# Causal convolution and spectral mix: x with two rows to a partition, and the convolution cut into quadrants of the array

## The chip, the cores and the metric

The kernel runs on one core of a Trainium2 chip. The metric is the device time of one execution in microseconds (us). Before the change the median of three runs is 177.64 us (177.45 to 178.16). A profiled execution gives the trace; its own time and span stand in the table below.

A core has five engines, each with its own queue: TensorE (PE in the profile; its weight loads are PEld), VectorE (DVE), ScalarE (ACT), GpSimd (POOL) and SyncE (SP). TensorE writes to eight banks of PSUM; VectorE and ScalarE move ("evict") results from PSUM to SBUF. Transfers run on 16 DMA engines; POOL issues the input transfers, which also turn float32 into bfloat16, and SP issues the output.

## The reference

```python
# x (8, 3264, 192); weight (8, 7); w_r, w_i (64, 192, 192); w_ch (192, 192)
w = softmax(weight, axis=-1)                          # 8 heads, 7 taps
x_pad = concat(zeros(B, 6, D), x)                     # causal
x = einsum('hk,bskhg->bshg', w, windows(x_pad))       # 24 columns per head
X = rfft(x, axis=1)[:, :64]                           # 64 modes
Yr = Xr @ w_r - Xi @ w_i                              # per mode
Yi = Xr @ w_i + Xi @ w_r
y = irfft(Y, n=S, axis=1)
u = x + y
out = u + maximum(u @ w_ch, 0)
```

## The kernel before

Batches go in four pairs `q`. A row block is 256 sequence rows; there are 13 to a batch (the last has 192), so 26 half blocks `t` of 128 rows or fewer. `xall` holds x in bfloat16 in slots of half blocks, both batches of a pair side by side, 192 columns each.

*Loading.* `load_unit` (L148) loads one unit of a pair in two transfers, one per batch. One x row goes to one partition: the packet is one row, 192 bfloat16, 384 bytes in SBUF. The short tails of all pairs come in two transfers (L236). The units are (first block, blocks): `UNITS0 = (0,2) (2,3) (5,4) (9,4)` for the first pair and `UNITS = (0,4) (4,4) (8,5)` for the others, 13 units in all. After x and `w_ch` POOL issues the mode weights (`load_w`, L264), two transfers of 288 KB for each of 16 groups of four modes. Eight groups have room from the start; each of the other eight is asked for once `mix(g)` of an earlier group has run.

*Front.* VectorE builds the banded tap matrix `band` (masks L178, softmax L180 to L190, seven predicated copies L193, copies to `band` L199 on ScalarE and L201 on VectorE). Meanwhile 30 filler products (`NIDLE`, L174) keep TensorE busy.

*Convolution.* `conv_pass` takes two heads of one unit: 16 products (L283) of a 128-row by 64-column tile of the array, two column halves side by side, into a PSUM tile of two banks. There are three such tiles in turn. The result goes back in place to `xall`, alternately through ScalarE (L290) and VectorE (L292); the rows come out so that even and odd rows lie in separate half blocks. Four passes make a unit.

*Fourier tables.* `table(step, t0, t1)` computes the cosines and sines in `ftab`: steps 0 to 2 on VectorE (L210, L213, L215), 3 to 5 on ScalarE (L217, L219, L221). The dictionary `extra` places these steps between the passes, in three parts of the table.

*Transform.* `dft` (L301) adds up the transform of a pair over its 26 half blocks, in two column halves of the array, in one of two banks kept for it. `dfts(n)` places five or six half blocks at a time between the passes. ScalarE copies the sum to `xs` (L305). `xtrans` (L316, L318) transposes it, and L325 and L327 copy it to `xt`.

*Mode products.* `mix(g)` (L426) multiplies four modes by their weights. Around it `some(n)` works off a list of transposes (L387, copied by L377 and L379) that the output stage needs. `mix(0)` needs the transform of all four pairs. Near the end `warm` (L580) puts filler products between the last mode products.

*Output stage.* From about 106 us products (L642), clamps (L558), additions (L545) and output transfers run interleaved over the 26 half blocks of each pair. The change doesn't edit it.

The order of instructions on each engine is the program's order (`manual_schedule`); only the waits are added by the framework.

Of the kernel before, what the change touches and what calls it, by code (L numbers as in the profile page):

```python
# [19 lines left out]
def kernel(  # L20
# [18 lines left out]
    NF = S // P  # L39
    HALF = S - NF * P  # L40
    NB = NF // 2 + 1
    NT = 2 * NB
    PL = (S - 2 * P * (NB - 1)) // 2
    NSLOT = NQ * NT + 1
    PW = 32 + KK - 1
    TWOPI = 6.283185
    MAGIC = 12582912.0
    NIDLE = 30
    UNITS0 = ((0, 2), (2, 3), (5, 4), (9, 4))
    UNITS = ((0, 4), (4, 4), (8, 5))  # L50
# [20 lines left out]
    band = shared[:, 0:H * 2 * P].rearrange("p (h c) -> p h c", h=H)  # L71
# [4 lines left out]
    ylate = sb("ylate", [2 * D], BF16)  # L76
# [5 lines left out]
    xs = [sb(f"xs{i}", [2, D], BF16) for i in range(2)]  # L82

# [21 lines left out]
    packed = temp(H * PW, BF16)  # L105
# [6 lines left out]
    wrec = temp(H, F32)  # L112
    cidx = temp(PW, F32)
    goff = temp(1, F32)
    masks = temp(KK * PW, U16)
# [20 lines left out]
    zl = open_psum("left", (2, 2))  # L136
    zr = open_psum("right", (1, 1, 2))
    ZC = [zl[0], zl[1], zr[2]]
    zf = zr[0:2]

    def load_unit(q, b0, n):
        t0 = 2 * b0
        nf = min(2 * n, NF - t0)
        s0 = NT * q + t0 + 1
        for i in range(2):
            off = ((2 * q + i) * S + P * t0) * D
            src = bass.AP(tensor=x.tensor, offset=x.offset + off, ap=[[D, P], [P * D, nf], [1, D]])
            nc.gpsimd.dma_start(out=xall[:, s0:s0 + nf, i, :], in_=src)  # L148
# [12 lines left out]
    load_unit(*units[2])  # L161
    nc.vector.memset(packed, 0.0)
    nc.vector.memset(xall[:, 0, :, :], 0.0)
    nc.scalar.copy(out=band[:, :, PW:2 * P], in_=packed[:, 0:1].unsqueeze(2).to_broadcast([P, H, 2 * P - PW]))
    nc.vector.memset(band[:, :, 0:PW], 0.0)
    for g in range(4):
        nc.vector.memset(goff[32 * g:32 * g + 32, :], float(32 * g))
    nc.vector.memset(xall[HALF:P, NT:NSLOT:NT, :, :], 0.0)
# [4 lines left out]
    for _ in range(NIDLE):  # L173
        nc.tensor.matmul(ZC[2][:, 0, :], zeros, zeros.unsqueeze(1).to_broadcast([P, 4, P]), start=True, stop=True,  # L174
                         skip_group_check=True)
    nc.vector.tensor_scalar(out=cidx[:, 0:PW], in0=cidx[:, 0:PW], scalar1=goff[:, 0:1], scalar2=None, op0=ALU.add)
    for k in range(KK):
        nc.vector.tensor_scalar(out=masks[:, PW * k:PW * (k + 1)], in0=cidx[:, 0:PW],  # L178
                                scalar1=float(KK - 1 - k), scalar2=None, op0=ALU.is_equal)
# [4 lines left out]
    nc.scalar.activation(out=wrec, in_=ascale.to_broadcast([P, H]), func=ACT.Sin)  # L184
# [6 lines left out]
    pk3 = packed.rearrange("p (h c) -> p h c", h=H)  # L191
    for k in range(KK):
        nc.vector.copy_predicated(out=pk3,  # L193
# [43 lines left out]
    for u in units[4:6]:  # L237
        load_unit(*u)
# [492 lines left out]
```

## Time and profile before

| | |
|---|---|
| median of three runs | 177.64 us |
| the profiled execution | 176.57 us |
| its span in the trace | 174.6 us |
| mean granted TensorE clock | 0.995 |
| TensorE matmul busy | 160.1 us (92%) |
| VectorE busy | 122.0 us (70%) |
| ScalarE busy | 106.9 us (61%) |
| first convolution product (L283) | 11.57 us |
| first mode product (L426) | 68.92 us |
| HBM read and written | 39.10 MB and 20.05 MB |

The times in the trace count from the span's start. A busy share is an average over stages with different limits; what a change in a stage is worth is read from the waits of that stage. Matmuls overlap, so TensorE's row in the slices tells that it has work, not that it runs at its peak. Each digit of a slice row is the busy share in tenths over a fortieth of the span (4.4 us). In the groups the two numbers after the bar are the union of busy time in us and the mean duration in ns, and behind the next bar stands the idle time of the engine just ahead of them with what ended it. A row of the windows has, after the stretch, the busy time of PE, PEld, DVE, ACT and POOL, the granted clock, the DMA share and GB/s.

### The profile page before, as it was taken

To read this page: it belongs to the slowest core of one execution; us is meant where nothing else is said; L and a number is where in the kernel's file an instruction comes from. 1 tells how busy PE (TensorE), PEld (TensorE's weight loads), DVE (VectorE), ACT (ScalarE), POOL (GpSimd) and SP (SyncE) were. 2 spreads that over 40 slices of the span, in tenths; PEclk is the share of its full clock that TensorE was granted. 3 is DMA by queue.
4 is the path that set the end of the run, shared out by engine and by line. 5 is a ranking of instruction groups with operands and counts; after the bars stand their busy time and mean duration, and the time that the engine had idled before them with its cause. 6 is when DMAs were issued, how large, how long until landed. Compare 5 with 4: busy or idle time off the path is not lost.

```text
span 174.6 us, 6593 instructions
## 1 busy us (share of the span) xinstructions
PE 160.1 (92%) x2756; PEld 139.7 (80%) x2756; DVE 122.0 (70%) x226; ACT 106.9 (61%) x191; POOL 58.6 (34%) x101
## 2 busy tenths in 40 slices
PE   7967999999999988999967978999999999999990
PEld 2447989999998966899966545599999999999960
DVE  5669883274454562777745225699999999999991
ACT  6337885434544342787645244588788888887870
POOL 7999943465322344424344000592000000000000
PEclk9999999999999999999999999999999999999998
DMA  4999999999999999999999980289989899999896
GB/s 46 168 188 192 191 194 192 191 192 193 193 193 194 203 206 207 205 207 206 206 207 206 207 147 9 70 301 327 367 305 341 334 332 360 341 343 333 324 345 226
DMA packets 50541, 40.11 MB, mean 230 GB/s; under 512 B 28720, under 2 KB 50512, under 8 KB 50512
## 3 DMA queue, kind: packets, MB, share of 16 engines
q0 software_dynamic: 36000, 19.62, 81.2%
q1 hardware_dynamic: 14512, 20.09, 31.5%
q8 instruction: 21, 0.34, 0.8%
q14 instruction: 8, 0.07, 0.1%
HBM read 39.10 MB, written 20.05 MB: 339 GB/s over the span
## 4 chain that ended last, share of the span: by engine, by line
PE 72%; DMA 13%; DVE 5%; ACT 4%; issue 2%; POOL 1%; DVEq 0%; POOLq 0%; ACTq 0%
PE z L642 33%; PE z L283 19%; DMA arena<-in_moe_w_i_dram 13%; PE z L301 10%; PE z L387 4%; DVE arena L193 2%; PE z L426 2%; ACT xall L290 1%; DVE xall L292 1%; PE z L569 1%; POOL xall L148 1%; PE z L512 1%; ACT L184 1%; DVE arena L545 1%; PE z L316 1%
## 5 line engine op out<-in xcount | busy, mean ns | idle before, releaser
L545 DVE TENSOR_TENSOR arena<-z,xall 128x384 f32<-128x384 f32 (+1 forms) x104 | 57.5, 557 | 3.1 <-PE z L642 1.1
L558 ACT ACTIVATE z<-z 128x384 f32<-128x384 f32 x102 | 48.3, 475 | 12.6 <-PE z L642 3.6
L642 PE MATMUL z<-arena,ftab 64*128 64x384 bf16 x308 | 45.3, 323 | 0.0
L642 PEld LDWEIGHTS <-ct 64*128 64x128 bf16 x600 | 42.4, 94 | 1.9 <-PE z L569 0.6
L642 PE MATMUL z<-wsw,ct 64*128 64x192 bf16 x300 | 42.2, 243 | 0.0
L283 PE MATMUL z<-xall,shared 128*64 128x192 bf16 (+3 forms) x832 | 39.1, 246 | 2.6 <-ACT shared L199 1.5
L283 PEld LDWEIGHTS <-shared 128*64 128x64 bf16 x832 | 36.3, 110 | 5.0 <-ACT shared L199 2.0
L292 DVE CAST xall<-z 128x768 bf16<-128x768 f32 (+3 forms) x26 | 24.8, 956 | 21.9 <-PE z L283 18.9
L642 PE MATMUL z<-wm,ct 64*128 64x192 bf16 x200 | 34.1, 243 | 0.0
L290 ACT CAST xall<-z 128x768 bf16<-128x768 f32 (+3 forms) x26 | 20.6, 795 | 19.4 <-PE z L283 19.3
L642 PEld LDWEIGHTS <-ftab 64*128 64x128 bf16 x396 | 26.6, 93 | 1.4 <-issue 0.8
L148 POOL DMA_DIRECT2D xall<-in_x_dram x26 | 23.7, 920 | 11.3 <-DMA xall<-in_x_dram 10.4
L642 PE MATMUL z<-w,ct 64*128 64x192 bf16 x100 | 24.3, 243 | 0.0
L379 DVE COPY ct<-z 128x1024 bf16<-128x1024 bf16 x26 | 17.1, 687 | 8.0 <-PE z L387 4.8
L301 PE MATMUL z<-xall,ftab 128*64 128x384 bf16 (+1 forms) x208 | 20.9, 326 | 0.7 <-ACT xall L290 0.7
L387 PE MATMUL z<-ident,xall 128*128 128x128 bf16 x312 | 19.3, 220 | 0.2 <-ACT ftab L377 0.2
L387 PEld LDWEIGHTS <-xall 128*128 128x128 bf16 x312 | 17.7, 98 | 0.9 <-issue 0.3
L377 ACT COPY ct<-z 128x1024 bf16<-128x1024 bf16 x13 | 13.2, 1012 | 4.2 <-PE z L387 4.0
L301 PEld LDWEIGHTS <-ftab 128*64 128x64 bf16 (+1 forms) x208 | 13.1, 110 | 2.6 <-DVE xall L292 0.6
L642 PE MATMUL z<-mixa,ftab 64*128 64x384 bf16 x88 | 13.8, 323 | 0.0
L453 POOL DMA_DIRECT2D arena<-ylate x16 | 7.9, 504 | 15.8 <-ACT ylate L449 15.8
L264 POOL DMA_DIRECT2D arena<-in_moe_w_r_dram x13 | 8.0, 613 | 14.9 <-PE z L387 5.7
(108 smaller groups left out, 133.4 us busy)
## 6 DMA issues: line engine op xcount, KB each, us to landing
out_dram<-arena SPq DMA_DIRECT2D x47, 384.0 KB, 3.4
xall<-in_x_dram POOLq DMA_DIRECT2D x14, 384.0 KB, 13.1
arena<-in_moe_w_r_dram POOLq DMA_DIRECT2D x13, 288.0 KB, 11.4
arena<-in_moe_w_i_dram POOLq DMA_DIRECT2D x13, 288.0 KB, 11.7
xall<-in_x_dram POOLq DMA_DIRECT2D x6, 432.0 KB, 13.6
ct<-in_moe_w_r_dram POOLq DMA_DIRECT2D x3, 288.0 KB, 11.8
ct<-in_moe_w_i_dram POOLq DMA_DIRECT2D x3, 288.0 KB, 11.3
out_dram<-arena SPq DMA_DIRECT2D x3, 288.0 KB, 3.6
```

Source lines behind the costliest of these rows:

```text
L148: nc.gpsimd.dma_start(out=xall[:, s0:s0 + nf, i, :], in_=src)
L264: nc.gpsimd.dma_start(out=wts[g][64 * half:64 * half + 64, :, :, :], in_=src[4 * g:4 * g + 4, :, :].rearrange("m (p j) e -> p m j e", j=3))
L283: nc.tensor.matmul(o, lhs, xall[:, r0:r0 + 2 * n - 1:2, :, dsl], start=(main and a == 0), stop=not main, tile_position=(0, 64 * half), ski ...
L290: nc.scalar.copy(out=dst, in_=srcv)
L292: nc.vector.tensor_copy(out=dst, in_=srcv)
L301: nc.tensor.matmul(xp[r, :], ftab[0:k, t, r], xall[0:k, NT * q + t, :, :], start=(t == 0), stop=(t == NT - 1), tile_position=(0, 64 * hh), ...
L377: nc.scalar.copy(out=out, in_=in_)
L379: nc.vector.tensor_copy(out=out, in_=in_)
L387: nc.tensor.matmul(o, in_, ident[:], start=True, stop=True, is_transpose=True)
L545: nc.vector.tensor_tensor(out=o[0:pn, :, a, :], in0=bank[0:pn, 0:2 * D].rearrange("p (i d) -> p i d", i=2), in1=xall[0:pn, s + a, :, :], o ...
L558: nc.scalar.activation(out=z, in_=z, func=ACT.Relu)
L642: mm = nc.tensor.matmul(target(bank[k], cols, r), l, r, start=first, stop=last, skip_group_check=True)
```

## The change

* A packet of x is now two rows: row pair `2p, 2p+1` of a block goes to partition `p`. The tail of each pair comes with its unit.
* Eight units of six or seven blocks in place of 13.
* The band is split by lag parity into two planes, for two heads' halves: heads 0 to 3 are built first and copied by ScalarE, then heads 4 to 7, copied by VectorE. `wsin` gets its own place.
* A step of the convolution is one head and one output parity `a`. It fills one bank of eight. The lower 64 input partitions give four products (two input parities, two column halves); the upper 64 give four more, issued two steps later, after a wait for the lower ones. Both steps of a head are evicted when the second is complete.
* The table has two parts instead of three; steps 0 to 3 of the first part stand ahead of the convolution.
* The transform of a pair comes in two parts, one for each unit, with the full array. The first part's sum goes to `xacc` through ScalarE, and VectorE adds the second part. For the first pair each unit ends with `flush()` and its part of the transform.
* 43 fillers at the front instead of 30, and four instead of seven in one `warm`.

```diff
-    NIDLE = 30
-    UNITS0 = ((0, 2), (2, 3), (5, 4), (9, 4))
-    UNITS = ((0, 4), (4, 4), (8, 5))
+    NIDLE = 43
+    UNITS0 = ((0, 6), (6, 7))
+    UNITS = ((0, 7), (7, 6))
...
+    xacc = ct[:, 0:6, :].rearrange("p t s -> p (t s)").bitcast(F32)
+    ylate = xs[0][:, :, :].rearrange("p i d -> p (i d)")
+    xin = xall[:, :, :, :].rearrange("p (b x) i d -> p b (x i d)", x=2)
+    xin5 = xin.rearrange("p b (i a d) -> p b i a d", i=2, a=2)
...
-    zl = open_psum("left", (2, 2))
-    zr = open_psum("right", (1, 1, 2))
-    ZC = [zl[0], zl[1], zr[2]]
-    zf = zr[0:2]
+    zl = open_psum("left", (1, 1, 1, 1))
+    zr = open_psum("right", (1, 1, 1, 1))
+    ZC = [z[:, 0, :] for z in zl + zr]
...
-            src = bass.AP(tensor=x.tensor, offset=x.offset + off, ap=[[D, P], [P * D, nf], [1, D]])
-            nc.gpsimd.dma_start(out=xall[:, s0:s0 + nf, i, :], in_=src)
+            src = bass.AP(tensor=x.tensor, offset=x.offset + off, ap=[[2 * D, P], [2 * P * D, nf], [1, 2 * D]])
+            nc.gpsimd.dma_start(out=xin[:, s0:s0 + nf, 2 * D * i:2 * D * (i + 1)], in_=src)
+        if nf < n:
+            off = (2 * q * S + 2 * P * (NB - 1)) * D
+            src = bass.AP(tensor=x.tensor, offset=x.offset + off, ap=[[2 * D, PL], [S * D, 2], [1, 2 * D]])
+            nc.gpsimd.dma_start(out=xin[0:PL, s0 + nf, :].rearrange("p (i c) -> p i c", i=2), in_=src)
...
-    nc.vector.memset(xall[HALF:P, NT:NSLOT:NT, :, :], 0.0)
+    nc.vector.memset(xin[PL:P, NB:NB * NQ + 1:NB, :], 0.0)
...
-    for k in range(KK):
-        nc.vector.copy_predicated(out=pk3,
-                                  mask=masks[:, PW * k:PW * (k + 1)].unsqueeze(1).to_broadcast([P, H, PW]),
-                                  data=ta3[:, :, k:k + 1].to_broadcast([P, H, PW]))
+    pk4 = packed.rearrange("p (h o c) -> p h o c", h=H, o=2)
+    for h0 in (0, H // 2):
+        hs = slice(h0, h0 + H // 2)
+        for lag in range(KK):
+            k = lag // 2
+            nc.vector.copy_predicated(
+                out=pk4[:, hs, lag % 2, :],
+                mask=masks[:, PW * k:PW * (k + 1)].unsqueeze(1).to_broadcast([P, H // 2, PW]),
+                data=ta3[:, hs, KK - 1 - lag:KK - lag].to_broadcast([P, H // 2, PW]))
+        for g in range(4):
+            c0 = 1 + 32 * (g % 2)
+            dst, srcv = band[32 * g:32 * g + 32, hs, :, c0:c0 + PW], pk4[32 * g:32 * g + 32, hs, :, :]
+            if h0 == 0:
+                nc.scalar.copy(out=dst, in_=srcv)
+            else:
+                nc.vector.tensor_copy(out=dst, in_=srcv)
...
+    def conv_pieces(step, row):
+
+        (q, b0, n, h, a), z = step
+        s0 = NB * q + b0 + 1
+        r = slice(64 * row, 64 * row + 64)
+        dsl = slice(GRP * h, GRP * h + GRP)
+        for a1 in range(2):
+            for col in (row, 1 - row):
+                c0 = (0 if a < a1 else 1) + (64 if col != row else 0)
+                s1 = s0 - 1 if (row, col) == (1, 0) else s0
+                o = z[64 * col:64 * col + 64, 0:2 * GRP * n].rearrange("p (b i e) -> p b i e", b=n, i=2)
+                yield nc.tensor.matmul(o, band[r, h, int(a != a1), c0:c0 + 64], xin5[r, s1:s1 + n, :, a1, dsl],
+                                       start=(row == 0 and a1 == 0), stop=(row == 1 and a1 == 1),
+                                       tile_position=(64 * row, 64 * col), skip_group_check=True).ins.name
...
+    CONVLAG = 2
+
+    def conv_step(u):
...
+        if u is not None:
+            flow[-1][1].extend(lower)
+        if old is not None:
+            turn(old[1][2:])
+            for _ in upper:
+                pass
+        if old is not None and old[0][0][4] == 1:
+            for (q, b0, n, h, a), z in (flow[-2 - CONVLAG][0], old[0]):
+                s0 = NT * q + 2 * b0 + a
+                dst = xall[:, s0:s0 + 2 * n - 1:2, :, GRP * h:GRP * h + GRP]
+                srcv = z[:, 0:2 * GRP * n].rearrange("p (b i e) -> p b i e", b=n, i=2)
+                if (2 * h + a) % 8 in (1, 4, 7) if (q, b0) == (0, 6) else a == 1:
+                    nc.scalar.copy(out=dst, in_=srcv)
+                else:
+                    nc.vector.tensor_copy(out=dst, in_=srcv)
+
+    def flush():
+        for _ in range(CONVLAG):
+            conv_step(None)
+        flow.clear()
...
+        xp = conv_bank()[:, 0:2 * D]
         for t in range(t0, t1):
             k = PL if t >= NT - 2 else P
-            for hh in range(2):
-                r = slice(64 * hh, 64 * hh + 64)
-                nc.tensor.matmul(xp[r, :], ftab[0:k, t, r], xall[0:k, NT * q + t, :, :],
-                                 start=(t == 0), stop=(t == NT - 1), tile_position=(0, 64 * hh),
-                                 skip_group_check=True)
-        if t1 == NT:
-            nc.scalar.copy(out=xs[q % 2][:], in_=xp.rearrange("p (i d) -> p i d", i=2))
+            nc.tensor.matmul(xp, ftab[0:k, t, :], xall[0:k, NT * q + t, :, :],
+                             start=(t == t0), stop=(t == t1 - 1), skip_group_check=True)
+        if t0 == 0:
+            nc.scalar.copy(out=xacc, in_=xp)
+        else:
+            nc.vector.tensor_tensor(out=xs[q % 2][:, :, :].rearrange("p i d -> p (i d)"), in0=xp, in1=xacc, op=ALU.add)
...
+    p1, p2 = (0, 12), (12, NT)
+    extra = {(0, 2): ((4, *p1),), (0, 4): ((5, *p1),), (0, 7): ((0, *p2), (1, *p2), (2, *p2), (3, *p2)),
+             (1, 2): ((4, *p2),), (1, 4): ((5, *p2),)}
...
+    for step in range(4):
+        table(step, *p1)
     for k, u in enumerate(units):
-        for h2 in range(4):
-            conv_pass(*u, h2)
-            for e in extra.get((k, h2), ()):
+        for h in range(H):
+            for a in range(2):
+                conv_step((*u, h, a))
+            for e in extra.get((k, h), ()):
                 table(*e)
-            if h2 == 1 and pend:
-                xtrans(pend.pop(0))
-            if k == 2 and h2 >= 2:
-                dfts(5)
-            elif k > 3 and h2 in (1, 3):
-                dfts(6)
-        if k == 4:
+            if k > 2 and h == 2:
+                if pend:
+                    xtrans(pend.pop(0))
+                dfts()
+        if k == 2:
             for g in range(NW + 3):
                 load_w(g)
         todo.append((u[0], 2 * u[1], 2 * (u[1] + u[2])))
-    dfts(99)
+        if u[0] == 0:
+
+            flush()
+            dfts()
+            if pend:
+                xtrans(pend.pop(0))
+    flush()
+    dfts()
...
-    warm(zm[1], 7)
+    warm(zm[1], 4)
```

## The prediction

> **What bounds the kernel now.** I read the slices first, then the chain of waits in order of time, then the waits of TensorE. The slices: rows TensorE, DMA share and GB/s of the page.
>
> ```profile
> PE   7967999999999988999967978999999999999990
> DMA  4999999999999999999999980289989899999896
> GB/s 46 168 188 192 191 194 192 191 192 193 193 193 194 203 206 207 205 207 206 206 207 206 207 147 9 70 301 327 367 305 341 334 332 360 341 343 333 324 345 226
> ```
>
> From 5 to 103 us the input transfers never pause: x at about 191 GB/s, then the mode weights at 207. The chain of waits shows the stages (start, length, what):
>
> ```profile
> 11.57 2.72 PE z L283 x96
> ...
> 23.69 1.51 PE z L283 x32
> ...
> 68.92 0.71 PE z L426 x23
> ...
> 79.89 11.78 DMA arena<-in_moe_w_i_dram
> ...
> 91.96 11.04 DMA arena<-in_moe_w_i_dram
> 103.00 0.04 issue
> 103.05 0.49 PE z L426 x10
> ```
>
> Convolution (L283) starts at 11.57; the second pair of batches starts near 23.7; the first mode product (L426, `mix(0)`) starts at 68.92. From 79.89 the chain is the weight transfers alone, so TensorE has slack there. The waits of TensorE say how much:
>
> ```profile
> PE z L426 <- DMA arena<-in_moe_w_i_dram: 2.7, 3, 1.5
> ```
>
> Only 2.7 us in three waits. The output stage after 106 us is full on TensorE, VectorE and ScalarE and is not edited. So two things set the end: the transfers, and 2.7 us behind them the start of `mix(0)`. A later `mix(0)` costs its delay less this slack.
>
> **The change, part by part.** Durations come from these groups (mean ns after the comma) and from two short windows:
>
> ```profile
> L292 DVE CAST xall<-z 128x768 bf16<-128x768 f32 x16 | 15.3, 957 | 13.5 <-PE z L283 11.1 <-ACT xall L290 1.7 <-ACT mixa L327 0.6
> L290 ACT CAST xall<-z 128x768 bf16<-128x768 f32 x16 | 12.6, 794 | 9.5 <-PE z L283 9.3
> ...
> L292 DVE CAST xall<-z 128x384 bf16<-128x384 f32 x2 | 1.1, 556 | 1.2 <-PE z L283 1.2
> ...
> L290 ACT CAST xall<-z 128x384 bf16<-128x384 f32 x2 | 1.0, 478 | 0.8 <-PE z L283 0.8
> ```
>
> ```profile
> 172.00:173.00 1.00, 0.00 (x0) 0.00 (x0) 0.00 (x0) 0.00 (x0) 0.00 (x0) 0.92 1.00 305
> 173.00:174.00 1.00, 0.00 (x0) 0.00 (x0) 0.00 (x0) 0.00 (x0) 0.00 (x0) 0.50 0.09 27
> ```
>
> *x transfers.* A packet grows from 384 to 768 bytes. Sixteen queues at 191 GB/s take 32.2 ns per 384 bytes, and at 207 GB/s 89.0 ns per 1152 bytes (weights); halfway, 60.6 ns, is 203 GB/s. x is 10.03 MB: 52.5 us becomes 49.5. Gain 3.0; ends 0 (rate stays) and 4.1 (weights' rate). It lies beside TensorE's work and is worth something only if `mix(0)` is not late.
>
> *Convolution products.* 832 of 64 output columns by 128 rows become 1,024 quadrants of 64 by 64; streamed columns per quadrant stay equal. Products of 96 columns start in pairs every 42.5 ns, of 192 every 82.5: columns/2.4 + 2.5 ns. A step (one head, one parity) has four products in each row half, two columns halves abreast, so 2 x 142.5 = 285 ns for seven blocks and 245 for six, if all four quadrants run together. 16 steps a unit: 4.56 and 3.92 us, 33.9 in all, as before. The transform: 104 products of 384 columns at 162.5 ns, 16.9, also as before. No gain here.
>
> *Evictions.* 52 become 128. The four rows above give 0.156 us + 1.043 ns per element on VectorE and 0.158 + 0.833 on ScalarE: 0.506/0.438 us for 336 elements, 0.456/0.398 for 288. A pair of steps (0.57 or 0.49) just covers them once nothing else is queued.
>
> *Shape changes of the array.* Before, L283, L301 and L316 share one tile shape. Now there are five changes a pair (quadrants, full array, column halves). From L426 to L387 the nearest such change leaves 0.10 us. 15 in the last three pairs: 1.5 us (ends 0 and 3).
>
> *The front.* 13 more fillers (L174) at 512/2.4 + 2.5 = 216 ns put the first convolution at 12.95 instead of 11.57. Walking VectorE's list: the memset of the x tail rows doubles (0.70 to an estimated 1.34), three masks go, the reciprocal no longer waits 1.0 for L184, and the 14 predicated copies are of 140 elements (0.30 each by the formula that gives 0.473 for L193's 304, measured 0.478). Half the band is ready at 10.6, all at 12.1. Then come the first three table steps, 768 elements each (0.95, 0.79, 0.95 by L210 at 0.817 and L213 at 0.659 for 640): VectorE can evict from 15.1, ScalarE after its sine of 1.06 from 16.2. The eight banks are full at 14.9, so TensorE waits; ScalarE's own order (two evictions, Abs 0.82, two evictions, Sin 1.19) paces the rest and unit 0's last product ends at 19.55, for 3.92 us of work.
>
> *Queued in front of the first transform.* This is the dearest edit. In program order the second table part (steps 0 to 3, 896 elements) stands after all 16 steps, but ahead of unit 0's last two evictions, which `flush()` issues. VectorE: 1.09 + 0.92 + 1.09 from 19.74 to 22.95, then its last eviction. ScalarE: the sine waits for them, 1.19 to 24.2, then its last eviction, to 24.6. The transform needs these slots, and unit 1's products stand behind it on TensorE although their x landed near 17. TensorE idles 5.1 us. Then 12 x 0.1625 = 1.95 of transform; unit 1 from 26.7, whose ten VectorE evictions take 10 x 0.526 from 27.98 to 33.3; 14 products of transform to 35.6; the addition and six transpose pairs: the second pair starts at 36.8, against 23.7 before.
>
> *Clock.* Before, matmuls ended near 170.1, and the granted clock is 0.92 in 172 to 173 and 0.50 after, so it falls after about 2.8 idle us. 5.1 idle us should halve it: the first transform costs up to 1.95 more and the convolution behind it some; part hides under the ten evictions. I take 1.8 (ends 0 and 2.7).
>
> *Three pairs more.* Convolution 25.4, transform 12.7, transposes 0.7, changes 1.5, waits for banks and the last evictions 2.0: last transform ends at 36.8 + 42.3 = 79.1. Addition, transposes and copy into `xt`: 2.1, as in before from 67.1 to 68.92 with one step more. `mix(0)` at 81.2, with the clock's 1.8 at 83.0: 14.1 us late. The same walk over the old program gives 68.7 where the trace has 68.92.
>
> *After mix(0).* The first eight weight groups have landed near 79. The other eight are asked for after each product on POOL's queue and need 2 x 1.42 us each, 23 in all: down by 107, while TensorE reaches `mix(14)` 31 us after `mix(0)`. So the 2.7 us of waits vanish, and three of seven fillers of `warm` (0.216 each), now not covered by a wait, save 0.65.
>
> **Sum**, against the profiled execution's own 176.57: 14.1 - 2.7 - 0.65 = +10.7, so 187.3. The median, 177.64, is 1.07 above that execution: forecast 188.3, given as 188. Without the clock's fall 186.5.
>
> **Rivals.**
> (a) *Faster: the first pair's waits are covered, and the transfers decide.* If evictions and tables fit under TensorE, it runs 12.95 + 33.9 + 16.9 + 1.3 + 2.3 + 3.0, `mix(0)` at 70.4, 1.5 late; 1.5 - 3.35 gives 174.7, 175.8 on the median's scale. It decides from a `mix(0)` before 72.2. For it: transfers lead the chain from 79.89. Against: the table steps stand ahead of evictions in both queues.
>
> (b) *In-order starts.* Each step issues four lower, then four upper products. If a product could not start past an earlier one of the other half, each step would gain four start distances, 7 to 21 ns (two loads and products every 42.5 ns): at 21, 85 ns x 96 steps = 8.2 us, 196. Against it, the output stage:
>
> ```profile
> 129.96 0.32 PE L642 MATMUL z<-arena,ftab 64*128 64x384 bf16 x1
> ...
> 130.53 0.32 PE L642 MATMUL z<-arena,ftab 64*128 64x384 bf16 x1
> ...
> 131.10 0.32 PE L642 MATMUL z<-arena,ftab 64*128 64x384 bf16 x1
> ```
>
> Each item there has 1344 columns a half, 560 ns, and the same product returns every 570 ns. Walked strictly in the order of issue it would be 640. So halves pass each other. [...]
>
> (c) *The quadrants do not run four abreast.* Two halves of rows and two halves of columns each overlap in the trace, but never all four. Two abreast would add 25 us in the last three pairs and some 4 in the first: 217.
>
> (d) *Smaller loss.* The first pair's waits are half as long: 181 to 184.
>
> **How the numbers follow.** Forecast 0.60 (184 to 191.5 with the ends of its terms), (a) 0.12, no change 0.04, (d) 0.10, (b) 0.10, (c) 0.04. A measurement tells 0.5%, 0.9 us, from no change. Range 181 to 196: it leaves out (a), (c) and no change. Faster 0.12, same 0.04, slower 0.84.
>
> **What would show it.** TensorE idle about 5 us between 19 and 25 us, ended by a ScalarE eviction; three 128x896 VectorE steps just before it; the clock digit below 9 there; the second pair's convolution from 36 to 39 us; TensorE full from there on; the first mode product at 81 to 84, and no wait of these products for weights. Steps of 285 ns in seven-block units prove the four quadrants. If the mode products still wait for weights, or the first starts before 72, the prediction is wrong.

## The result and the profile after

| | before | after |
|---|---|---|
| median on one chip, four runs each | 177.54 us | 185.38 us (185.18 to 186.88) |
| the profiled execution | 176.57 us | 185.26 us |
| its span in the trace | 174.6 us | 183.5 us |
| mean granted TensorE clock | 0.995 | 0.987 |
| second pair's convolution starts | 23.69 us | 35.45 us |
| first mode product, `mix(0)` | 68.92 us | 81.60 us |
| last group of x has landed | 59.04 us | 55.31 us |

The ratio of the times is 1.0453, with a 95% interval of 1.0392 to 1.0513. The change makes the kernel slower by 4.5%. The profiled execution was forecast at 187.3 and took 185.26. Three of the four runs of after took 185.18 to 185.49 us at a mean granted clock of 0.987 or 0.988, and one took 186.88 at 0.971; the last section says what can explain it.

The slices of the page of after, to be laid beside the three rows of before:

```profile
PE   6998198899999999869999998899999999999990
PEclk9999879999999999999999999999999999999998
GB/s 42 202 203 204 203 204 203 203 202 204 201 205 208 207 206 207 169 2 128 196 205 126 137 196 61 0 147 313 360 329 347 345 343 329 346 340 318 352 348 210
```

x now moves at 203 GB/s (191 before) and is down 3.7 us earlier. TensorE has a hole in the fifth slice (18.3 to 22.9 us, digit 1), and the clock digits of this slice and the next are 8 and 7. Later, from about 77 us, the transfers pause (2 and 128 GB/s), since the weights now wait for TensorE. The chain of waits of after in order of time (start, length, what) shows what filled the hole:

```profile
17.64 0.46 DVE xall L332
18.09 1.01 DVE arena L224
19.13 0.64 DVE arena L227
19.79 1.10 DVE arena L229
20.91 1.20 ACT ftab L231
22.11 0.25 ACT xall L330
22.40 3.33 PE z L344 x11
...
35.52 5.43 PE z L300 x138
...
81.60 0.71 PE z L469 x23
```

L224 to L231 are the second table part's steps 0 to 3, L330 is unit 0's last eviction on ScalarE, L344 the first transform, L300 the convolution, L469 `mix`. From 18.09 to 22.11 the chain runs through table work that this transform does not need. It then takes 3.33 us for 11 products, which is 0.30 us a product instead of 0.1625, and the windows of after tell why (stretch, its length, busy time of PE, PEld, DVE, ACT, POOL, granted clock, DMA share, GB/s):

```profile
18.38:21.79 3.41, 0.32 (x1) 0.10 (x1) 2.80 (x4) 1.26 (x3) 1.45 (x2) 1.00 1.32 203
21.79:25.21 3.42, 2.81 (x9) 1.28 (x9) 0.00 (x0) 0.56 (x2) 0.92 (x2) 0.50 1.31 203
25.21:28.62 3.41, 3.41 (x79) 2.72 (x81) 1.41 (x3) 2.03 (x4) 0.60 (x2) 1.00 1.32 203
```

The clock is 1.00, then 0.50 for 3.42 us, then 1.00 again.

At the other end, the waits of after hold no wait of L469 for a transfer. It is the weights' transfers that wait for L469 (first row), and L469 waits once, for a copy into `mixa`:

```profile
POOL arena L273 <- PE z L469: 28.2, 5, 14.4
...
PE z L469 <- ACT mixa L369: 1.4, 1, 1.4
```

`mix(0)` to `mix(14)` takes 30.21 us in after (81.60 to 111.81) and took 34.13 before: 3.92 us of the 12.68 us come back there. What follows `mix(14)` takes 71.68 and took 71.51. So 12.68 - 3.92 + 0.17 = 8.93 us, the difference of the two spans.

The last step ahead of `mix(0)` is longer than forecast. The timeline of after shows VectorE there:

```profile
79.67 0.79 DVE L413 MEMSET z<- 128x384 f32 x2
...
80.37 0.67 DVE L422 COPY ftab<-z 128x1024 bf16<-128x1024 bf16 x1
80.96 0.54 DVE L367 CAST mixa<-z 128x384 bf16<-128x384 f32 x1
...
81.60 0.63 PE L469 MATMUL z<-arena,mixa 128*16 128x192 bf16 x20 [1.41 <-ACT mixa L369]
```

The wait is put down to ScalarE's half of the copy (L369), but that was done at 80.71. VectorE's half, L367, ends last, at 81.50. It stands behind two memsets (L413) and a copy (L422), and these follow the addition that ends the last transform (L349, on VectorE as well; before, a copy on ScalarE stood there).

### The profile page after: what moved, and what is told of

Same layout as the page of the kernel before. It is cut to its first block, busy times and chain, and to the rows that moved or that the text cites. A ratio compares the mean times of both kernels' runs of the same rounds, so it can differ in the third digit from the quotient of the medians.

```text
span 183.5 us, 6844 instructions
## 1 busy us (share of the span) xinstructions
PE 166.2 (91%) x2854; PEld 132.5 (72%) x2854; DVE 131.6 (72%) x273; ACT 111.4 (61%) x226; POOL 51.9 (28%) x93
## 4 chain that ended last, share of the span: by engine, by line
PE 76%; DVE 14%; ACT 4%; issue 3%; DVEq 0%
PE z L678 32%; PE z L300 14%; PE z L430 11%; PE z L344 10%; DVE xall L332 4%; PE z L469 3%; DVE arena L205 2%; DVE arena L229 1%; DVE arena L224 1%; PE z L358 1%; PE z L548 1%; PE z L605 1%; PE z L539 1%; DVE xall L175 1%; DVE arena L227 1%
## 5 line engine op out<-in xcount | busy, mean ns | idle before, releaser
L332 DVE CAST xall<-z 128x336 bf16<-128x336 f32 (+1 forms) x66 | 31.1, 483 | 19.8 <-PE z L300 11.7
L300 PE MATMUL z<-xall,shared 64*64 64x336 bf16 (+1 forms) x1024 | 38.7, 294 | 1.2 <-DVE xall L332 0.7
L300 PEld LDWEIGHTS <-shared 64*64 64x64 bf16 x1024 | 32.9, 106 | 7.0 <-issue 4.3
L678 PE MATMUL z<-wsw,ct 64*128 64x192 bf16 x300 | 37.5, 243 | 0.0
L330 ACT CAST xall<-z 128x288 bf16<-128x288 f32 (+1 forms) x62 | 25.4, 419 | 13.1 <-PE z L300 9.0
L678 PE MATMUL z<-wm,ct 64*128 64x192 bf16 x200 | 31.4, 243 | 0.0
L344 PE MATMUL z<-xall,ftab 128*128 128x384 bf16 (+1 forms) x104 | 19.8, 342 | 5.4 <-DVE xall L332 4.7
L422 DVE COPY ct<-z 128x1024 bf16<-128x1024 bf16 x26 | 17.0, 687 | 5.2 <-PE z L430 4.0
L344 PEld LDWEIGHTS <-ftab 128*128 128x128 bf16 (+1 forms) x104 | 10.1, 101 | 13.9 <-issue 7.3
L151 POOL DMA_DIRECT2D xall<-in_x_dram x16 | 14.4, 905 | 8.9 <-DMA xall<-in_x_dram 8.1
L181 PE MATMUL z<-xall 128*128 128x512 bf16 x43 | 11.0, 422 | 1.6 <-DVE xall L169 1.6
```

The costliest lines, as they stand in the source:

```text
L151: nc.gpsimd.dma_start(out=xin[:, s0:s0 + nf, 2 * D * i:2 * D * (i + 1)], in_=src)
L181: nc.tensor.matmul(ZC[6], zeros, zeros.unsqueeze(1).to_broadcast([P, 4, P]), start=True, stop=True, skip_group_check=True)
L300: yield nc.tensor.matmul(o, band[r, h, int(a != a1), c0:c0 + 64], xin5[r, s1:s1 + n, :, a1, dsl], start=(row == 0 and a1 == 0), stop=(row ...
L330: nc.scalar.copy(out=dst, in_=srcv)
L332: nc.vector.tensor_copy(out=dst, in_=srcv)
L344: nc.tensor.matmul(xp, ftab[0:k, t, :], xall[0:k, NT * q + t, :, :], start=(t == t0), stop=(t == t1 - 1), skip_group_check=True)
```

## The experiments

"The second pair" below is the start of its convolution. Each run is compared with runs of the kernel before on the same chip (medians 176.97 to 177.26 us).

### The second table part moved behind unit 1's first steps

```diff
-    extra = {(0, 2): ((4, *p1),), (0, 4): ((5, *p1),), (0, 7): ((0, *p2), (1, *p2), (2, *p2), (3, *p2)),
-             (1, 2): ((4, *p2),), (1, 4): ((5, *p2),)}
+    extra = {(0, 2): ((4, *p1),), (0, 4): ((5, *p1),), (1, 0): ((0, *p2), (1, *p2)),
+             (1, 1): ((2, *p2), (3, *p2)), (1, 3): ((4, *p2),), (1, 5): ((5, *p2),)}
```

> The changed kernel with one edit: steps 0 to 3 of the second table part stand in unit 1 instead of ahead of unit 0's last evictions. Theory (work queued in front of the first transform): TensorE's gap of 3.26 and 0.78 us around 18 to 22 us falls below 1.5, the granted clock stays full, the second pair's first convolution product comes near 32 instead of 35.45 (the table steps now lengthen unit 1 on VectorE by 2.8), and the time falls by 3 to 4 us from 185.4, to 181.5 to 182.5. Rival (unit 1 waits for its x or for its own evictions anyway): less than 0.7 us.

182.60 us, ratio 1.0321 (1.0288 to 1.0355), just above the expected 181.5 to 182.5. The first transform in the timeline of this run:

```profile
18.53 0.32 PE L344 MATMUL z<-xall,ftab 128*128 128x384 bf16 x1 [0.55 <-DVE xall L332]
19.05 1.95 PE L344 MATMUL z<-xall,ftab 128*128 128x384 bf16 x11 [0.20 <-ACT xall L330]
```

The 3.26 and 0.78 us of idle time are 0.55 and 0.20 here, the clock does not fall, and the 11 products take 1.95 us instead of 3.31 in the timeline of after. The second pair starts at 32.30 in place of 35.45. The same steps in another place give 3.15 us back: the queue in front of the last two evictions, with the clock it takes down, is shown. It is 1.3 of the 4.5%, and not the whole.

### Fourteen fillers ahead of the first transform

```diff
+            if k == 0:
+                zb = conv_bank()
+                for _ in range(14):
+                    nc.tensor.matmul(zb, zeros, zeros.unsqueeze(1).to_broadcast([P, 4, P]), start=True, stop=True,
+                                     skip_group_check=True)
```

> The changed kernel with 14 filler products on TensorE ahead of the first transform, no other edit. Theory (the idle gap halves the clock and this costs time of its own): the clock stays full, the first transform takes 1.95 instead of 3.3 us, the second pair starts 1.3 to 1.7 us earlier, time near 183.8. Rival (the slower transform hides under the ten VectorE evictions of unit 1): no change within 0.3 us. The table steps still stand in front, so the transform's start near 22 stays.

184.64 us, ratio 1.0437 (1.0406 to 1.0468), between the expected 183.8 and no change. The first transform in this run:

```profile
22.24 1.95 PE L344 MATMUL z<-xall,ftab 128*128 128x384 bf16 x11 [0.68 <-ACT xall L330]
```

It still starts late, but the clock stays full and the second pair starts at 33.93, 1.52 us earlier. That is the price of the clock's fall; the prediction had taken 1.8. Only 0.85 us of it reach `mix(0)`, at 80.75. The fillers take one bank of the ring of eight, all later steps sit one bank further on, and a wait of 0.50 us that after does not have stands at 39.42. An edit that is only meant to fill a hole also moved the ring.

### The halves issued in turn

```diff
-        if u is not None:
-            flow[-1][1].extend(lower)
...
-            for _ in upper:
-                pass
+        for _ in range(4):
+            if u is not None:
+                flow[-1][1].append(next(lower))
+            if old is not None:
+                next(upper)
```

> The changed kernel with lower and upper products issued alternately instead of four and four. Theory (products of the two row halves start independently of their order of issue): steps stay at 285 and 245 ns, time within 0.3 us of 185.4. Rival (starts in the order of issue): alternating takes out four start distances a step, 10 to 30 ns, 1 to 3 us over the last three pairs.

186.66 us, ratio 1.0542 (1.0506 to 1.0578), so not within the 0.3 us expected. From the second pair to `mix(0)` it takes 46.05 us, and 46.15 in after. So whether four lower and four upper products are issued in blocks or in turn made a difference of 0.10 us here: a product starts past an earlier one of the other row half. The trace of after shows it directly at the start of the second pair, counted from its first product (35.45). The two halves are told apart there by their chains of starts, each 142 ns apart. The first upper products of the first step start at 0.54 us, but the first lower products of the third step, which stand ahead of them in program order, at 0.60.

What the median lost is mostly the clock. In this run's trace it turned full at 6.58 us (4.73 in after), the first unit started at 13.44 (12.52), and the clock was halved for 6.83 us, so the second pair started at 36.38; that is 0.93 of the 1.1 us by which the span grew. Three of its four runs had a mean clock of 0.971 or 0.972 and took 186.36 to 187.13, as after did with 186.88 at 0.971; the one at 0.988 took 185.94.

### x in 384-byte packets again

```diff
-            off = ((2 * q + i) * S + 2 * P * b0) * D
-            src = bass.AP(tensor=x.tensor, offset=x.offset + off, ap=[[2 * D, P], [2 * P * D, nf], [1, 2 * D]])
-            nc.gpsimd.dma_start(out=xin[:, s0:s0 + nf, 2 * D * i:2 * D * (i + 1)], in_=src)
+            for a in range(2):
+                off = ((2 * q + i) * S + 2 * P * b0 + a) * D
+                src = bass.AP(tensor=x.tensor, offset=x.offset + off, ap=[[2 * D, P], [2 * P * D, nf], [1, D]])
+                nc.gpsimd.dma_start(out=xin5[:, s0:s0 + nf, i, a, :], in_=src)
```

> The changed kernel with the same layout of x, but each transfer split by row parity, so that a packet is 384 bytes again and there are twice as many x transfers. Theory (x is off the path once TensorE is late): x lands near 59 instead of 55.3 us, time within 0.5 us of 185.4. Rival (the transfers still pace the first pair or the mode weights): up to 3 us slower.

187.76 us, ratio 1.0618 (1.0583 to 1.0653). x lands at 58.69 as expected, but the time is not within the 0.5 us expected. From the second pair to `mix(0)` it takes 46.35 us (46.15), so the later x costs 0.2 us there. The loss is in the front: the second pair starts at 38.70, 3.25 us later. (The profiled execution took 188.96; the other three runs took 187.62 to 187.88.) The timeline of GpSimd in this run has

```profile
1.27 3.49 POOL L152 DMA_DIRECT2D xall<-in_x_dram  x4 [0.83 <-POOLq L752]
4.81 0.23 POOL L162 IOTA arena<- 128x35 f32 x1
4.94 3.34 POOL L152 DMA_DIRECT2D xall<-in_x_dram  x4
...
8.89 0.34 POOL L165 IOTA arena<- 128x26 f32 x1
```

where after has the two iotas at 3.19 and 5.65. Masks, band and tables wait for them. Twice as many transfers stand ahead of them on the same queue, at about 0.9 us each. The next run puts the iotas first:

```diff
-    load_unit(*units[0])
     nc.gpsimd.iota(cidx[:, 0:PW], pattern=[[1, PW]], base=0, channel_multiplier=-1,
...
-    load_unit(*units[1])
     nc.gpsimd.iota(sidx.rearrange("p (b a) -> p b a", a=2), pattern=[[2 * P, NB], [1, 2]], base=0,
...
+    load_unit(*units[0])
+    load_unit(*units[1])
```

> The same 384-byte packets as in the run before with 36 transfers of x, but with GpSimd's three iotas issued ahead of all transfers. If what that run lost was the order on GpSimd's queue (its iotas at 4.81 and 8.89 us in place of 3.19 and 5.65, and with them masks, band, tables and the second pair, 38.70 in place of 35.45), the second pair starts again at 35.2 to 36.0 us and the time is 185 to 186 us, that of the changed kernel, although x lands 3.4 us later (about 58.7). If the short packets themselves cost time in this kernel, the time stays near 187.7 us.

186.77 us, ratio 1.0555 (1.0515 to 1.0596), second pair at 36.04. The first transform, with long packets at 21.30 after 3.26 us of idle time, in the run with the iotas behind and in this one:

```profile
22.87 0.48 PE L345 MATMUL z<-xall,ftab 128*128 128x384 bf16 x1 [3.26 <-DVE xall L333]
```

```profile
21.31 0.32 PE L345 MATMUL z<-xall,ftab 128*128 128x384 bf16 x1 [3.25 <-DVE xall L333]
```

So the order on GpSimd's queue cost 1.57 of the 3.25 us. The rest goes with the half clock behind it, which lasted 6.83 us (22.82 to 29.64) in the first of the two traces and 3.41 (22.79 to 26.20) in the second. Runs at like mean clock, 0.986 to 0.988, show the same order of size: with the iotas behind 187.62 to 187.88 us, with the iotas first 186.30 and 186.40, after 185.18 to 185.49.

The time is 0.8 us above what was expected. The profiled execution (186.30) is 1.04 us above that of after. Of this, 0.59 us lie before the second pair, though the first transform starts at the same time: the half clock ended at 26.20 instead of 25.21, and unit 1's convolution took 5.88 us instead of 5.34. That leaves some 0.4 us for the short packets themselves.

### The upper rows one step behind instead of two

```diff
-    CONVLAG = 2
+    CONVLAG = 1
```

> The changed kernel with the upper rows of a step one step behind the lower rows instead of two. Theory: the two row halves run beside each other, and with one step of distance the wait of the upper rows for the lower rows of the same step falls just behind the issue of the next lower rows, so it costs little: second pair to mix(0) 46.0 to 47.5 us (46.15 with two steps), time 185 to 187 us. Rival: the wait is exposed at each of the 128 steps (30 to 70 ns), and second pair to mix(0) takes 49 to 53 us, time above 188.5 us.

187.58 us, ratio 1.0597 (1.0539 to 1.0655). From the second pair to `mix(0)`: 48.09 us, between the two expectations. The 16 steps of a unit of seven blocks, in after and in this run:

```profile
50.98 4.60 PE L300 MATMUL z<-xall,shared 64*64 64x336 bf16 x128
```

```profile
53.66 5.03 PE L300 MATMUL z<-xall,shared 64*64 64x336 bf16 x128
```

The eight products of a step of seven blocks start over 285 ns in nearly all steps of after, and here over 310 in about half of them; for six blocks over 270 or more instead of 245 in most. So the wait shows, mostly with 25 ns where it does, 1.9 us in three pairs. The other 1.8 us of this trace are the front and the clock again (second pair at 37.23, clock halved for 6.83 us); the profiled execution took 189.16, and the other three runs, at a higher mean clock, 187.32 to 187.61. The second step of distance is a part of the change that pays.

### The first pair treated like the others

```diff
-            if k > 2 and h == 2:
-                if pend:
-                    xtrans(pend.pop(0))
+            if h == 2 and pend:
+                xtrans(pend.pop(0))
+            if k > 0 and h == 4:
+                dfts()
...
-        if u[0] == 0:
-
-            flush()
-            dfts()
-            if pend:
-                xtrans(pend.pop(0))
```

The twelve table steps are spread over both units, one or two at a time, 32 fillers stand in front instead of 43, and ScalarE takes the odd parity's eviction everywhere.

> The changed kernel with its first pair treated like the other three: no flush and no transform between its units and the second pair, its transform after the fifth group of passes of the following unit, and the twelve table steps spread one or two at a time over both units. Theory: the whole loss sits in the front (35.45 us at the second pair against 23.69 before), and the quadrant passes themselves cost no more than the old ones. Then four pairs of about 14.3 us each from 12.5 us end the last transform at 69 to 71 us, mix(0) starts at 71 to 73 us, the clock does not fall, and with x landed at 55 us the time is 175.5 to 177.5 us, at or below that of before. Rival: the shape changes and the quadrant passes cost the PE more per pair than the old form did; then mix(0) stays above 75 us and the time above 178.5 us.

179.85 us, ratio 1.0121 (1.0059 to 1.0184): the largest gain of all, but it stays above before. As the rival said, `mix(0)` stays above 75 us (76.50) and the time above 178.5. Several things change at once here, so the gain isn't split among them. The next run moves the two memsets in addition:

```diff
-        nc.vector.memset(z[:, 0:2 * D], 0.0)
+        nc.scalar.activation(out=z[:, 0:2 * D], in_=wm[:, 0:2 * D], func=ACT.Copy, scale=0.0)
```

> As the run with the first pair treated like the others, and the two memsets of accumulation banks ahead of mix(0) moved from VectorE to ScalarE. Theory: they stand on VectorE ahead of the copy that mix(0) waits for, so mix(0) comes 0.5 to 0.9 us earlier, and the time is lower by the same as long as products, not transfers, set the end: 174.5 to 176.8 us. Rival: transfers set the end, and nothing changes (within 0.3 us).

179.00 us (177.46 to 179.97), ratio 1.0102 (1.0044 to 1.0160); the time is above the expected span, the shift of `mix(0)` is as expected. From the first transpose to `mix(0)` it takes 1.12 us (73.90 to 75.02) and 1.95 in after, so the memsets had cost 0.83. `mix(0)` is at 75.02, 6.1 us behind before, and from there to the end it takes 101.98 us against 105.64. Of the 6.1 us, 3.1 come between the second pair and `mix(0)` (48.32 us against 45.23). That fits what a later pair costs: 14.27 us in after (its transposes start at 55.51 and 69.78) and 13.32 before (43.51 and 56.83), some 2.9 us over three pairs. Of the 0.95 a pair, 0.35 are a wait for a bank, and the five shape changes can be most of the rest: in after's trace the next product starts 0.07 to 0.10 us later there than within a shape. That was not tried by itself.

The other 3.0 us stand ahead of the second pair (26.70, before 23.69), and their parts are estimates from the trace. The clock is at half for 3.41 us from 18.68 though TensorE was busy all through it, at most 1.7 us. TensorE's waits in the first pair are 2.4 us, of which 1.01 for x of the second unit; before has one of 0.9 there (at 16.40). The first pair is itself one of the longer ones (0.95), and it starts 1.17 us earlier than before's: 1.7 + 1.5 + 0.95 - 1.17 = 3.0. The four runs follow the mean clock: 177.46 us at 0.993, 178.81 at 0.987, 179.18 at 0.983 and 179.97 at 0.981.

### With 384-byte packets on top

> As the run with the memsets on ScalarE, but with 384-byte packets of x (two transfers for one) and the iotas ahead of all transfers. Theory: in the changed kernel the faster x was off the path, because TensorE came 12.7 us late; once TensorE keeps up, x's last landing (58.7 in place of 55.3 us) moves the weights and the end with it: 2.0 to 3.4 us slower than with 768-byte packets. Rival: products still set the end, and the packet size costs less than 0.7 us.

The iotas stand first here as well. 180.02 us, ratio 1.0146 (1.0103 to 1.0189): 1.0 us slower, with overlapping ranges, and between the two expectations. x ends 3.4 us later (58.54), and `mix(0)` starts at 75.21, 0.19 later. That is not the price of the packets, because the clock differs: this trace lost none of it in the first pair, and the one with long packets was at half for 3.41 us. Against that, its first unit starts at 11.57 instead of 10.40, behind fillers that ran longer at half clock (first rise at 7.59, there 5.02), and from the second pair to `mix(0)` it takes 48.92 us instead of 48.32. At a mean clock of 0.983 the runs took 179.76 and 180.29 here, and 179.18 there. So by these runs the faster x is worth about 1 us once TensorE comes earlier, and whether products or transfers set the end stays open.

### Other units in the first pair, and tables on GpSimd

Units of 4, 5 and 4 blocks in place of 6 and 7:

```diff
-    UNITS0 = ((0, 6), (6, 7))
+    UNITS0 = ((0, 4), (4, 5), (9, 4))
```

> As the run with the first pair treated like the others and the memsets on ScalarE, but the first pair in three units of 4, 5 and 4 blocks. In that run the second unit (7 blocks) could not start before its x had landed (17.85 us), TensorE idled 2.4 us between 13.5 and 18 us, and the second pair started at 26.7 us. Theory: x of the first pair, at about 1 us a block, bounds the front; with smaller units the second pair starts 2 to 4 us earlier (22.5 to 24.5 us), mix(0) comes at 71 to 73 us and the time falls to 174.5 to 176.5 us, at or below that of before. Rival: the evictions and table steps of small units bound the front instead, and the second pair does not come earlier than 26 us: 178 to 180 us.

The table's two parts are cut anew in this run and the next two. 182.14 us, ratio 1.0274 (1.0202 to 1.0346): the rival holds. The third unit starts at 20.68, but evictions behind table steps of up to 1.6 us, and once a table step itself, stop TensorE for 0.57 to 0.78 us at a time, and the clock falls at 24.73. Units of 8 and 5 blocks, behind 43 fillers:

```diff
-    UNITS0 = ((0, 6), (6, 7))
+    UNITS0 = ((0, 8), (8, 5))
...
-    NIDLE = 32
+    NIDLE = 43
```

> As the run with the first pair treated like the others and the memsets on ScalarE, but the first pair in units of 8 and 5 blocks, and 43 fillers in place of 32, so that the first unit starts when all its x has landed (about 12.5 us) and TensorE then has no gap for x. Theory: one pair costs TensorE some 14.3 us in this form whatever stands ahead of it, so the second pair starts at 24 to 25.5 us, mix(0) comes at 72 to 74 us and the time is 175.5 to 177.5 us. Rival: the evictions or tables stand in front of the first transform again, and the second pair starts after 26 us (178 us or more).

180.70 us, ratio 1.0202 (1.0153 to 1.0251). Again the rival: the second pair starts at 29.52. The timeline of TensorE in this run:

```profile
19.45 0.53 PE L300 MATMUL z<-xall,shared 64*64 64x384 bf16 x8 [0.75 <-DVE xall L332]
20.68 1.38 PE L300 MATMUL z<-xall,shared 64*64 64x384 bf16 x32 [0.70 <-ACT xall L330]
...
24.43 0.84 PE L300 MATMUL z<-xall,shared 64*64 64x240 bf16 x24 [0.91 <-ACT xall L330]
```

x has landed (17.13) and it is only evictions that end these waits. The last run takes the first three table steps from VectorE to GpSimd:

```diff
-            nc.vector.tensor_tensor(out=tu, in0=sidx[:, t0:t1].unsqueeze(2).to_broadcast([P, n, MODES]),
+            nc.gpsimd.tensor_tensor(out=tu, in0=sidx[:, t0:t1].unsqueeze(2).to_broadcast([P, n, MODES]),
...
+    for step in range(3):
+        table(step, *p1)
+    load_unit(*units[2])
+    load_unit(*units[3])
+    for step in range(3):
+        table(step, *p2)
```

> As the run with units of 8 and 5 blocks, but the first three steps of both table parts (index times mode, rounding, difference) on GpSimd, ahead of x's third transfer and behind the fourth, and ScalarE's three steps of the first part around the start of the first unit, of the second part under the first transform. There TensorE idled 3.3 us in the first pair behind evictions that stood behind table steps. Theory: these steps on the two evicting engines, not x and not the quadrant products, hold the first pair; without them the second pair starts at 24 to 25.5 us (29.52 there), mix(0) at 71 to 72.5 us (76.49 there), and the time is 174 to 176 us, below that of before. Rival: GpSimd's own steps end so late (after 14 us) that ScalarE's sines hold the evictions as before, or its later issue of x makes TensorE wait for x: 178 us or more.

179.34 us (six runs), ratio 1.0123 (1.0085 to 1.0161). The second pair starts at 28.04, only 1.5 us earlier (the first unit started 0.8 us later, at 13.78, by the chance of the clock that the last section shows), and the rival holds in its first half: GpSimd's steps on the first part take from 6.59 to 14.80 us, and x's last landing slips to 58.98. TensorE's waits between 13.8 and 25.2 us do shrink, from 3.3 us to 0.49, but one of 1.04 follows at 27.79, for an eviction behind ScalarE's steps of the second part. And single copies of VectorE stood still beside GpSimd's steps, which the last section also shows. None of these versions has a median below before.

## Why the prediction was right, step by step

*What bounds before.* Right: the 2.7 us of weight waits vanished, and mode products no longer wait for transfers.

*x transfers.* 203 GB/s forecast and measured. Off the path as said: with short packets and the iotas first, some 0.4 us are left that are not the clock. Where TensorE comes 6 us earlier they cost about 1 us by the medians, with overlapping ranges.

*Convolution and transform.* Steps of 285 and 245 ns forecast, and measured in most steps, so the four quadrants run abreast and rival (c) falls. Rival (b), in-order starts, falls with the run that alternates the halves and with the starts in the trace of after. Three pairs took 43.4 us (35.45 to 78.84) where 42.3 was forecast. The two ScalarE rows of the evictions give 0.162 us and 0.823 ns per element, not 0.158 and 0.833; for 336 and 288 elements that changes nothing.

*The front.* Right in its mechanism, too long in size. The second pair was forecast at 36.8 plus a clock loss of 1.8, and started at 35.45 with the loss in it: 3.15 us less, and ahead of the 36 to 39 that it named as a sign. Unit 0's last product was forecast to end at 19.55 and ended at 18.04; the first transform goes on at 22.40 instead of 24.6, which is 2.2 of the 3.15 us. The step that failed is the walk along VectorE's list with whole durations, one after the other. The 14 predicated copies do last 0.30 us each, but they take 3.10 us together, 0.22 from start to start, since the next begins under the tail of the last. The band is complete at 10.8 instead of 12.1. In the same way the ten evictions before the second transform take 4.5 us, not 5.3, at a mean duration of 0.50. The middle table step took 0.63 and not 0.92. The first unit's start, forecast at 12.95 and measured at 12.52, is the chance of the clock (last section), and it paid nothing: in the run with the iotas first that unit starts at 13.01 and the first transform at 21.31, in after at 21.30.

*The queue in front of the first transform.* Right in place and kind. TensorE idled 3.26 + 0.78 us (5.1 forecast), behind three 128x896 steps, as the prediction said it would look. The longer wait is ended by VectorE's last eviction and only the shorter by ScalarE's, where it named ScalarE alone. The run with the steps moved confirms it with 3.15 us. The waits were not half as long as forecast, so rival (d) with its 181 to 184 falls too.

*Clock.* Forecast at 1.8, shown to be 1.5. Its reason, a fall after about 2.8 idle us, was too simple (last section), and that half clock lasted 3.4 us in the profiled execution and not 6.8 was chance.

*The step ahead of `mix(0)`.* Forecast at 2.1, measured 2.76 (78.84 to 81.60). What was missed is the same kind of queue in front as in the first transform: the memsets, hidden before, now stand behind the addition.

*After `mix(0)`.* 3.35 us forecast back, 3.92 measured.

*Sum.* -3.15 (front and clock) + 1.09 (three pairs) + 0.66 (tail) = -1.40 us at `mix(0)`, 81.60 in place of 83.0; with -0.57 + 0.17 behind it, 1.8 us below the forecast in the span, 2.0 in the execution. Errors of both signs cancelled a part.

*Rival (a).* It needed `mix(0)` before 72.2 with all waits of the first pair covered. The versions that cover them best reach 75.0: in none of those tried do evictions, tables and x of the first pair fit under 12 us of products, and each later pair is 0.95 us longer. Its price of 175.8 was reached by none.

## What to carry to other kernels

Where work that a later stage needs is put into the list of an engine that also empties banks, count what stands behind it on that engine: here 4 us of tables held two evictions, these held the transform, and the hole took the clock down. Two edits meant for something else, more transfers ahead of an iota and an addition on VectorE ahead of memsets, cost some 1.6 and 0.8 us in the same way. The faster x was worth some 0.4 us while TensorE came late, and about 1 us once it came 6 us earlier. When walking an engine's list, take the distance of starts (0.22 us for the predicated copies) and not the durations (0.30). Before two traces are subtracted, compare their granted clocks: here a fall one window longer looked like 1.7 us of an edit's price.

## What the runs showed of the hardware

**The granted clock changed at multiples of 3.41 us.** In the traces of before and after all changes of the granted clock lie whole multiples of 3.413 us behind the first rise: 5.59 and 172.85 us in before, 4.73, 21.79, 25.21 and 182.22 us in after. A hole did not have to be long. The run with the memsets moved lost the clock at 18.68 without an idle stretch above 1.01 us (its windows):

```profile
15.27:18.68 3.41, 1.59 (x36) 1.10 (x39) 2.42 (x5) 3.41 (x7) 3.34 (x8) 1.00 1.32 204
18.68:22.09 3.41, 3.41 (x57) 2.99 (x50) 2.00 (x4) 1.60 (x4) 1.56 (x2) 0.50 1.31 203
```

A window of the run with the iotas first kept it:

```profile
15.96:19.37 3.41, 1.95 (x51) 1.34 (x41) 2.92 (x6) 2.82 (x7) 2.56 (x3) 1.00 1.54 194
```

Of such windows at full clock, those in which TensorE was busy for 0.32 us (18.38 to 21.79, after), 0.64 (169.43 to 172.85, before), 0.70 (19.37 to 22.79, iotas first), 1.59 (above) and 1.74 (73.34 to 76.75, the first pair treated like the others) ended in half clock; those with 1.89 (9.01 to 12.42, before), 1.95 (above) and 2.00 (79.82 to 83.23, after) kept it, and so did all others of before and after with more. At half clock a window with 2.81 busy us went back to full (21.79 to 25.21, after). So in these traces about half a window decided a fall, and how a hole of 2 to 4 us falls on the windows is chance: half clock lasted 3.41 us in after and 6.83 in the run with short packets, and TensorE's long wait was 3.26 us in both. It can also explain the run of after that took 186.88 us at a mean clock of 0.971.

The first rise also moved the start of the convolution, since a fixed number of fillers stands ahead of it. In after the fillers start 427 ns apart before the rise (4.73) and 216 behind it, and take 10.97 us. The 43 fillers of the runs with 8 and 5 blocks (rise at 5.62) and with the tables on GpSimd (7.28):

```profile
1.62 11.41 PE L181 MATMUL z<-xall 128*128 128x512 bf16 x43 [1.62 <-DVE xall L169]
```

```profile
1.62 12.23 PE L210 MATMUL z<-xall 128*128 128x512 bf16 x43 [1.62 <-DVE xall L198]
```

The first unit starts at 12.96 and 13.78, and at 12.52 in after: the 0.44 and 1.26 us are, within 0.02, half of what the rise comes behind 4.73.

**GpSimd beside VectorE.** The 14 predicated copies and the four band copies of VectorE while GpSimd only issues transfers (the run with 8 and 5 blocks; shortest, median and longest in ns):

```profile
L205 DVE COPY_PREDICATED arena<-arena x14: 298/300/309, 6.6 to 9.4; 128x140 bf16<-128x140 uint16 x14
```

```profile
L215 DVE COPY shared<-arena x4: 224/226/230, 9.8 to 10.5; 32x280 bf16<-32x280 bf16 x4
```

and beside the table steps on GpSimd (the last run):

```profile
L234 DVE COPY_PREDICATED arena<-arena x14: 293/295/1995, 6.7 to 12.0; 128x140 bf16<-128x140 uint16 x14
```

```profile
L244 DVE COPY shared<-arena x4: 226/461/2324, 12.3 to 15.2; 32x280 bf16<-32x280 bf16 x4
```

The median of the predicated copies did not move, so they did not become slower: single ones stood still. GpSimd's three steps and the two longest copies in that run's timelines:

```profile
6.59 1.90 POOL L176 TENSOR_TENSOR arena<-arena 128x1024 f32<-128x1024 f32 x1
8.58 3.79 POOL L179 TENSOR_SCALAR arena<-arena 128x1024 f32<-128x1024 f32 x1
12.46 2.34 POOL L181 TENSOR_TENSOR arena<-arena 128x1024 f32<-128x1024 f32 x1
```

```profile
6.66 2.00 DVE L234 COPY_PREDICATED arena<-arena 128x140 bf16<-128x140 uint16 x1
```

```profile
12.56 2.32 DVE L244 COPY shared<-arena 32x280 bf16<-32x280 bf16 x1
```

Each of the two starts just behind a GpSimd step with two input tensors and ends just behind that step's end. Under the middle step, with one input tensor, one predicated copy takes 1134 ns and eleven more run at their usual pace. With one band copy of 692 ns, these four cost VectorE 5.1 us. They did not delay the start of the first unit (13.78): ScalarE's half of the band was complete at 12.57, and the fillers ended later. What stopped the four copies is not shown, and spans on GpSimd are rough. Moving these steps from VectorE to GpSimd was not free, though in the run with 8 and 5 blocks GpSimd only issues transfers at that time.
